# Emitting a fused sparse-attention and gated-MLP kernel in beats of one 512-wide score tile, with DMA transposes for k and x, staged q and separate PSUM banks for the MLP

## The chip, the cores and the metric

The kernel runs on one core of a Trainium2 chip. The metric is the time of one execution on the device, in microseconds (us). A core has a matrix engine (PE), a vector engine (VectorE, DVE in the profile), a scalar engine (ScalarE, ACT), a general engine (GpSimd, POOL), a queue engine (SyncE, SP) and 16 DMA engines. The order of each engine's instructions is laid out when the program is built. In the traces of this case, a wait at the head of an engine's order holds what stands behind it: VectorE, for one, stood 4.80 us before a copy whose data was late, with a ready instruction next in line (shown below).

Runs carry a state, fast or slow. A slow run is one over 1.5% above the fastest of the same kernel.

## The reference

There are 4 batches of 8 heads, 768 positions and 64 channels. Each query scores the 32-key chunks by an upper bound made from the minimum and maximum of k in the chunk, keeps the 6 best chunks, and does causal attention over them. The heads are joined to x (768 x 512 per batch), which goes through a gated MLP with a mixing step along the sequence.

```python
ub = np.sum(np.maximum(q[:, :, :, None, :] * k_min[:, :, None, :, :],
                       q[:, :, :, None, :] * k_max[:, :, None, :, :]), axis=-1)
ub = np.where(causal, ub, -1000000000.0)
top_chunks = np.argsort(ub, axis=-1)[..., -top_k:]
...
scores = np.where(mask, scale * np.matmul(q, k.transpose(0, 1, 3, 2)), -1000000000.0)
attn = softmax(scores)
x = (attn @ v), heads joined
...
h = np.maximum(x @ w_in, 0.0)                  # 512 -> 1024
u, v = h[..., :512], h[..., 512:]
v_n = (v - mean(v)) / sqrt(var(v) + 1e-06)
v_s = np.einsum('ts,bsd->btd', w_spatial, v_n) + b_spatial[None, :, None]
return (u * v_s) @ w_out
```

## The kernel before

The kernel works in 16 pairs of heads. `load` fetches the pair's k, q and v (float32 in memory, float16 in the tile) in six DMA transfers. `prep` transposes k on PE, finds chunk minima and maxima, transposes q, makes bounds, selects chunks, writes the selection into the free half of the padded q tile, and transposes both heads' query operands (`a`). `attend` makes scores in tiles of up to 1,024 columns, with the causal triangle added by a small product, takes the exp, and multiplies by the values. The MLP of batch b is cut into pieces and handed out over the pairs of batch b+1.

```python
ps_sc = ctx.enter_context(tc.psum_pool(name="ps_sc", bufs=2))    # tiles of 1024 columns: 4 banks
ps_tr = ctx.enter_context(tc.psum_pool(name="ps_tr", bufs=2))
ps_acc = ctx.enter_context(tc.psum_pool(name="ps_acc", bufs=2))  # bounds, values and the whole MLP
...
def load(i):
    for hi in range(2):
        ...
        nc.gpsimd.dma_start(out=kp[:, :, hi, :], in_=view(k))
        nc.gpsimd.dma_start(out=qs[:, :, hi, c0:c0 + D], in_=view(q))   # straight into the padded tile
        nc.gpsimd.dma_start(out=vt[:, :, hi, 0:D], in_=view(v))

def prep(i):
    tr = trans_tile()
    for t in range(NQT):
        nc.tensor.transpose(tr[:, t * P:(t + 1) * P], kp[:, t, :, :], identity)
    ... # kmm: chunk max and min of tr, on VectorE
    nc.scalar.copy(kh[0][D:2 * D, :], tr[0:D, :])
    nc.scalar.copy(kh[1][0:D, :], tr[D:2 * D, :])
    for m in range(2):
        nc.gpsimd.tensor_tensor(km[:, m], ..., op=Alu.mult)              # on POOL
    ... # q transposed, its positive and negative parts, bounds, top 8, selection
    for hi in range(2): ... # a: six transposes and a VectorE copy

def attend(i):
    for hi in range(2):
        for g, strips in enumerate(STRIPS):                              # 1024, 1024, 640 columns
            for (t, q0, n, col, dg) in strips:
                mm(sc[:, col:col + n], lhsT=kh[hi][:, t * P:(t + 1) * P], rhs=a[hi][:, q0:q0 + n], ...)
                if dg:
                    mm(sc[:, col:col + P], lhsT=identity, rhs=tri, start=False, stop=True)
            nc.scalar.activation(out=e[...], in_=sc[:, 0:WIDTHS[g]], func=Act.Exp, scale=scale)
        ... # values on PE, normalised into x16 by VectorE
    ... # six PE transposes of x16, VectorE copy into xT

load(0); load(1)
load_weights()                # w_in, w_spatial, w_out, on the POOL queue
prep(0)
for i in range(NPAIR):
    load(i + 2); prep(i + 1); attend(i)
    ... # a share of the MLP pieces of the batch before
```

The softmax here doesn't subtract the row's maximum and nothing guards it: scores larger than these inputs give would overflow.

## Time and profile before

| | before |
|---|---|
| time, median of 4 runs beside the changed kernel | 292.24 us (291.39 to 294.32) |
| span of the profiled execution | 287.5 us |
| first exp of the attention | 27.5 us |
| first exp of pair 4 (batch 1 begins) | 78.0 us |
| first MLP result (batch 0) | 86.9 us |
| first MLP result of batch 3 | 257.1 us |
| instructions on PE | 2,340 |

A result of the MLP counts from the moment when ScalarE begins to copy it out of PSUM (tile `vraw`). The time to the first MLP result of batch 0, the time from there to the first of batch 3, and the rest (the last MLP alone) divide the span into 86.9 + 170.2 + 30.4 us. The middle part is called "the twelve pairs" below, as it holds three MLPs spread over twelve pairs. It is not exactly the attention of pairs 4 to 15 (pairs are counted from 0): pair 4 has its first exp at 78.0 us, before the first MLP result.

These are lines of the page of before. The digits are the busy tenths of 40 slices of 7.2 us each. "PEclk" is the PE clock that was granted.

```profile
PE 222.4 (77%) x2340; PEld 144.9 (50%) x2340; DVE 170.7 (59%) x498; ACT 154.3 (54%) x217; POOL 98.1 (34%) x150
...
PE   0037028787879798989798989978888989799994
...
DMA  0999997879996667558984848079220000140005
...
PE 50%; ACT 23%; DMA 8%; POOL 7%; DVE 7%; issue 3%; ACTq 0%; DVEq 0%; POOLq 0%
```

No engine is full. The last line shares out the chain of waits, followed back from the end: PE and ScalarE alternate. PE's row has a zero in the fifth slice (28.8 to 36 us).

The table by stretches of the same profile gives, after each stretch's length, the busy time of each engine, then the granted PE clock, the mean busy share of the DMA engines over the stretch (as a sum of overlapping packets, so it may pass 1) and the GB/s moved.

```profile
core 0: us, PE busy (x) PEld busy (x) DVE busy (x) ACT busy (x) POOL busy (x), PEclk, DMA share, GB/s
0.00:46.00 46.00, 12.65 (x110) 9.30 (x111) 18.49 (x57) 8.23 (x9) 31.83 (x51) 0.85 1.16 112
...
207.00:257.00 50.00, 45.09 (x443) 28.19 (x440) 29.01 (x80) 29.68 (x44) 1.88 (x5) 1.00 0.10 26
257.00:287.50 30.50, 25.24 (x133) 12.67 (x130) 12.33 (x26) 10.98 (x22) 0.00 (x0) 1.00 0.18 67
```

In the stretch from 207 to 257 us, PE is busy for 45.1 of 50 us. What is missing there is waiting. From 0 to 46 us, PE does 12.7 us of work. The timeline of PE shows the hole. Each line has start, length, and in brackets how long the engine was idle before it and what released it.

```profile
28.86 0.22 PE L213 MATMUL sc<-a_213,kh_0_92 128*128 128x128 f16 x1
40.09 0.20 PE L177 MATMUL acc<-km,rq 128*128 128x48 f16 x1 [11.01 <-POOL km L161]
```

PE waits 11 us for a small product `km` on POOL, and POOL stands, in its own order, at three load issues that in the trace wait in turn for w_in, ws_raw and w_out to land (3.5, 5.4 and 1.3 us). Why loads of q, k and v have to wait for weights is not shown. The waits view adds up such waits (total, times, longest).

```profile
POOL kp L140 <- PE tr L152: 48.0, 9, 9.7
...
ACT e L217 <- PE sc L216: 42.9, 31, 12.0
```

ScalarE waits 42.9 us in all for scores (12.0 of them in the hole just shown), in a kernel where PE waits too. So for part of the time the two engines take turns rather than work side by side.

### The profile page before, as it was taken

The page shows a single profiled execution, that of the slowest core. Times are in us where ns is not written, and L with a number is a line of the kernel's source. Part 1 is how long each engine was busy: PE and PEld are TensorE (multiplying, and loading weights), DVE is VectorE, ACT ScalarE, POOL GpSimd, SP SyncE. Part 2 cuts the span into 40 slices and gives each one's busy share as a digit, 9 for nine tenths or more (in the row PEclk, how much of TensorE's full clock was granted, in tenths as well). Part 3 has the DMA queues.
Part 4 walks back from the last instruction along what each step waited for, and adds up shares of the span by engine and source line. Part 5 has one row for each costly group of instructions (what it writes and reads, how often), then busy time and mean ns, then how long its engine had stood idle before and what let it go on. Part 6 is the DMA issues. An engine that isn't in the chain of part 4 may idle for free.

```text
span 287.5 us, 5812 instructions
## 1 busy us (share of the span) xinstructions
PE 222.4 (77%) x2340; PEld 144.9 (50%) x2340; DVE 170.7 (59%) x498; ACT 154.3 (54%) x217; POOL 98.1 (34%) x150
## 2 busy tenths in 40 slices
PE   0037028787879798989798989978888989799994
PEld 0025016666655565655465656655546565544551
DVE  8337005888788875565579865474688654238330
ACT  1021405775785868146878674086878660656213
POOL 9995264546562434124243424051200000000000
PEclk9999758999999999999999999999999999999999
DMA  0999997879996667558984848079220000140005
GB/s 1 65 120 199 194 127 52 56 49 71 70 65 41 46 41 47 37 64 65 204 55 31 55 31 57 0 81 222 16 15 3 0 2 0 39 182 2 0 0 219
DMA packets 80590, 18.86 MB, mean 66 GB/s; under 512 B 75698, under 2 KB 76978, under 8 KB 80564
## 3 DMA queue, kind: packets, MB, share of 16 engines
q0 software_dynamic: 77104, 12.20, 57.3%
q1 hardware_dynamic: 3460, 6.30, 6.0%
q8 instruction: 18, 0.29, 0.4%
q14 instruction: 8, 0.07, 0.1%
HBM read 24.39 MB, written 6.29 MB: 107 GB/s over the span
## 4 chain that ended last, share of the span: by engine, by line
PE 50%; ACT 23%; DMA 8%; POOL 7%; DVE 7%; issue 3%; ACTq 0%; DVEq 0%; POOLq 0%
ACT e L217 13%; PE acc L322 11%; PE sc L213 7%; PE acc L310 7%; DMA w_out_sb<-in_moe_w_out_dram 6%; PE acc L224 5%; PE acc L333 5%; PE acc L285 5%; DVE stats L289 2%; PE tr L234 2%; POOL kp L140 2%; PE sc L216 2%; DMA out_dram<-o 2%; ACT uT L312 2%; PE acc L324 2%
## 5 line engine op out<-in xcount | busy, mean ns | idle before, releaser
L217 ACT ACTIVATE e<-sc 128x1024 f16<-128x1024 f32 (+1 forms) x96 | 84.0, 916 | 44.0 <-PE sc L216 42.9
L140 POOL DMA_DIRECT2D kp<-in_k_dram x32 | 26.7, 839 | 54.1 <-PE tr L152 48.0
L224 PEld LDWEIGHTS <-e 128*128 128x128 f16 x672 | 27.0, 98 | 31.3 <-ACT e L217 17.8
L216 PE MATMUL sc<-tri,identity 128*128 128x128 f16 x192 | 39.5, 222 | 0.0
L336 ACT COPY o<-acc 128x512 f32<-128x512 f32 x24 | 14.0, 585 | 46.9 <-PE acc L333 44.8
L322 PE MATMUL acc<-wsT,vn 128*128 128x512 f16 (+1 forms) x192 | 37.2, 325 | 0.4 <-ACT uT L312 0.2
L325 DVE TENSOR_TENSOR gT<-acc,uT 128x512 f16<-128x512 f32 (+1 forms) x32 | 17.8, 557 | 20.0 <-PE acc L324 18.8
L155 DVE TENSOR_REDUCE kmm<-tr 128x24 f16<-128x768 f16 x16 | 15.3, 953 | 20.4 <-PE tr L152 20.3
L322 PEld LDWEIGHTS <-vn 128*128 128x128 f16 x192 | 18.2, 98 | 12.2 <-issue 1.1
L310 PE MATMUL acc<-xT,w_in_sb 128*128 128x512 f16 (+1 forms) x128 | 23.4, 325 | 0.9 <-ACT uT L312 0.7
L333 PE MATMUL acc<-w_out_sb,gT 128*128 128x512 f16 x96 | 23.1, 378 | 0.4 <-ACT o L336 0.3
L216 PEld LDWEIGHTS <-identity 128*128 128x128 f16 x192 | 19.0, 99 | 7.4 <-issue 5.7
L285 PE MATMUL acc<-w_in_sb,xT 128*128 128x512 f16 x96 | 22.2, 379 | 0.0
L177 PE MATMUL acc<-km,rq 128*128 128x48 f16 x160 | 9.6, 188 | 15.9 <-POOL km L161 14.5
L152 PE MATMUL tr<-identity,kp 128*128 128x128 f16 x96 | 10.0, 229 | 14.7 <-DMA kp<-in_k_dram 14.6
L312 ACT ACTIVATE uT<-acc 128x512 f16<-128x512 f32 (+1 forms) x32 | 14.3, 488 | 12.4 <-PE acc L310 12.3
L289 DVE BATCH_NORM_STATS2 stats<-vraw 128x6 f32<-128x512 f32 x24 | 16.6, 694 | 6.1 <-ACT vraw L287 6.1
L227 DVE RECIPROCAL rec<-acc 128x6 f32<-128x6 f32 x32 | 6.1, 190 | 22.9 <-PE acc L224 22.9
L287 ACT ACTIVATE vraw<-acc 128x512 f32<-128x512 f32 x24 | 14.3, 597 | 9.6 <-PE acc L285 9.6
L180 DVE TENSOR_TENSOR acc<-acc,cmask 128x40 f32<-128x40 f32 x16 | 3.3, 208 | 25.6 <-PE acc L177 22.7
L161 POOL TENSOR_TENSOR km<-kmm,hmask 128x48 f16<-128x48 f16 x32 | 8.3, 276 | 26.3 <-DVE kmm L155 22.6
L310 PEld LDWEIGHTS <-w_in_sb 128*128 128x128 f16 x128 | 12.1, 97 | 9.7 <-issue 1.3
(236 smaller groups left out, 452.0 us busy)
## 6 DMA issues: line engine op xcount, KB each, us to landing
out_dram<-o SPq DMA_DIRECT2D x24, 256.0 KB, 2.0
kp<-in_k_dram POOLq DMA_DIRECT2D x32, 96.0 KB, 3.3
qs_90<-in_q_dram POOLq DMA_DIRECT2D x12, 96.0 KB, 3.3
vt_96<-in_v_dram POOLq DMA_DIRECT2D x12, 96.0 KB, 3.0
ws_raw<-in_moe_w_spatial_dram POOLq DMA_DIRECT2D x1, 1152.0 KB, 15.1
w_in_sb<-in_moe_w_in_dram POOLq DMA_DIRECT2D x1, 1024.0 KB, 10.3
qs_98<-in_q_dram POOLq DMA_DIRECT2D x10, 96.0 KB, 3.2
vt_104<-in_v_dram POOLq DMA_DIRECT2D x10, 96.0 KB, 3.1
```

What stands on the lines that cost most here:

```text
L140: nc.gpsimd.dma_start(out=kp[:, :, hi, :], in_=view(k))
L213: mm(sc[:, col:col + n], lhsT=kh[hi][:, t * P:(t + 1) * P], rhs=a[hi][:, q0:q0 + n], start=True, stop=not dg)
L216: mm(sc[:, col:col + P], lhsT=identity, rhs=tri, start=False, stop=True)
L217: nc.scalar.activation(out=e[:, BASES[g]:BASES[g] + WIDTHS[g]], in_=sc[:, 0:WIDTHS[g]], func=Act.Exp, scale=scale)
L224: mm(avv[:, qi, :], lhsT=e[:, c:c + P], rhs=vt[:, t, hi, 0:D + 1], start=(t == 0), stop=(t == qi))
L285: mm(hv, lhsT=x[:, ko, bi * P:(bi + 1) * P], rhs=w_in_sb[:, ko, DH:DFF], start=(ko == 0), stop=(ko == NDO - 1))
L289: nc.vector.bn_stats(stats, st["vraw"][:, bi, :])
L310: mm(hu[:, 0:t1 - t0], lhsT=w_in_sb[:, ko, db * P:(db + 1) * P], rhs=x[:, ko, t0:t1], start=(ko == 0), stop=(ko == NDO - 1))
L312: nc.scalar.activation(st["uT"][:, db, t0:t1], hu[:, 0:t1 - t0], func=Act.Relu)
L322: mm(vs[:, 0:t1 - t0], lhsT=st["vn"][:, si, db * P:(db + 1) * P], rhs=wsT[:, si, t0:t1], start=(si == 0), stop=False)
L325: nc.vector.tensor_tensor(st["gT"][:, db, t0:t1], in0=vs[:, 0:t1 - t0], in1=st["uT"][:, db, t0:t1], op=Alu.mult)
L333: mm(o_ps, lhsT=st["gT"][:, db, ti * P:(ti + 1) * P], rhs=w_out_sb[:, db, :], start=(db == 0), stop=(db == KO - 1))
```

## The change

The intent is to keep PE fed. The whole kernel is emitted in beats, one for each 512-wide score tile (12 a pair), and in each beat a small share of every other stage is placed: preparation of coming pairs up to 27 beats ahead, values, and two matmuls or so of the MLP. The parts are:

- scores in six tiles of up to 512 columns with three one-bank buffers, in place of three tiles of 1,024 with two double-bank buffers;
- k and x transposed by the DMA engines (30 of the 32 transposes), q and `a` still by PE;
- q loaded into a staging tile and placed into the padded tile by two VectorE copies, so that loads can cover four heads at once (27 transfers of q, k and v in place of 96);
- kh copies moved from ScalarE to VectorE, `a` copies from VectorE to ScalarE, `km` from POOL to VectorE;
- the causal triangle cut out of e by POOL from the second batch on, in place of products on PE;
- three PSUM banks for the MLP, one for the values, one for transposes and bounds.

```diff
-STRIPS = [
-    [(0, 0, 512, 0, True), (1, 128, 512, 512, True)],
...
+TILES = [
+    [(0, 0, 512, 0)],
+    [(1, 128, 512, 0)],
+    [(2, 256, 512, 0)],
+    [(3, 384, 384, 0), (1, 640, 128, 384)],
+    [(4, 512, 256, 0), (0, 512, 256, 256)],
+    [(5, 640, 128, 0)],
+]
...
-    ps_sc = ctx.enter_context(tc.psum_pool(name="ps_sc", bufs=2))
-    ps_tr = ctx.enter_context(tc.psum_pool(name="ps_tr", bufs=2))
-    ps_acc = ctx.enter_context(tc.psum_pool(name="ps_acc", bufs=2))
+    ps_sc = ctx.enter_context(tc.psum_pool(name="ps_sc", bufs=3))
+    ps_tr = ctx.enter_context(tc.psum_pool(name="ps_tr", bufs=1))
+    ps_acc = ctx.enter_context(tc.psum_pool(name="ps_acc", bufs=1))
+    ps_ml = ctx.enter_context(tc.psum_pool(name="ps_ml", bufs=3))
...
+        def q_place(self):
+            nc.vector.tensor_copy(self.qs[:, :, 0, D:2 * D], self.q[:, 0])
+            nc.vector.tensor_copy(self.qs[:, :, 1, 0:D], self.q[:, 1])
+
+        def k_transpose(self):
+            src = self.k.rearrange("p h t d -> p (h t d)")
+            if self.i == 0:
+                ... # on PE
+            else:
+                kT = sb.tile([P, 2, NQT // 2, P], F16, tag="kT", name="kT")
+                nc.sync.dma_start_transpose(out=kT.rearrange("d h m s -> d (h m) s"), in_=src)
...
+        def k_operand(self, hi):
+            d0, d1 = HALF[1 - hi]
+            dst = self.kh[hi][d0:d1].rearrange("d (p m s) -> d p m s", p=2, s=P)
+            for sp, (s0, s1) in enumerate(HALF):
+                nc.vector.tensor_copy(dst[:, sp], self.kT[s0:s1, hi])
...
+        def triangle(self, hi, g0):
+            if self.b == 0:
+                return                                  # batch 0: product on PE, as before
+            e = self.e[hi]
+            blk = bass.AP(e.tensor, e.offset + g0 * 512, [list(e.ap[0]), [512, 3], [1, P]])
+            nc.gpsimd.affine_select(out=blk, in_=blk, compare_op=Alu.is_ge, fill=0.0, ...)
...
+        def x_transpose(self):
+            if self.i < NPAIR - 1:
+                nc.sync.dma_start_transpose(out=dst..., in_=self.x16...)
+            else:
+                ... # on PE
...
+    for g, group in enumerate(groups):
+        if g >= 2:
+            t0 = group[0] * BEATS
+            at(t0 - 36, load, "k", g, group)
+            at(t0 - 34, load, "q", g, group)
+            at(t0 - 16, load, "v", g, group)
...
+        at(t0 - 22, p.q_place)
+        at(t0 - 27, p.k_transpose)
+        at(t0 - 22, p.k_max)
+        at(t0 - 21, p.q_transpose)
...
+        at(t0 - 12, p.select)
...
+    at(1 * BEATS, load_w_in)
+    at(2 * BEATS, load_w_spatial)
+    at(3 * BEATS, load_w_out)
...
+    for b in range(B):
+        steps = mlp(b)
+        first, count = (b + 1) * HP * BEATS + 9, HP * BEATS
+        total, done = sum(c for c, _ in steps), 0
+        for cost, fn in steps:
+            at(first + done * count // total, fn)
+            done += cost
```

## The prediction

> **What bounds it now.** No engine does. The page gives PE 77% busy, VectorE 59%, ScalarE 54% and the chain of waits alternates: PE 50%, ScalarE 23%, DMA 8%, POOL 7%. By stretches (timeline):
>
> - Start, 0 to 46 us. POOL builds masks until 8 us, then issues the first k load; PE starts at 14.6, the first exp at 27.5. PE idles from about 29 to 40: POOL, in order, holds load issues until the weight loads land (w_out takes 16.9 us), with small `km` products behind them.
> - Batch 0 attention, to 86 us: about 12 us a pair.
> - Batches 1 to 3 with the previous batch's MLP: 60, 61 and 50 us, 14.2 a pair.
> - MLP of batch 3 alone, 256 to 287.5.
>
> PE's work per pair in the third stretch, from issue intervals in the timeline (216 ns per 512 columns, 56 per transpose, 34 per 65-column product), is about 12.4 us. Nearly 2 us is waiting: bounds, values and MLP share two `acc` banks (waits view: ScalarE 42.9 us for scores).
>
> **The change, per pair with MLP (estimated).**
>
> - PE: k and x transposes leave (-0.7), triangle products become POOL selects from batch 1 (-0.64): 11.0 us.
> - ScalarE: twelve exps instead of six. 1024 columns took 1.02 us and 640 took 0.70, so 512 is 0.60 and 128 is 0.27: 6.5 us instead of 5.5. Copies of kh (2 x 0.79) leave, of a arrive. With MLP: 10.8 us.
> - VectorE: loses a copies (1.1) and x copy (0.55), gains q, kh and bounds copies (about 1.5): 10.6 us, unchanged.
> - POOL: 96 input loads become 27; four selects a pair (0.45 each), off the path unless behind an issue.
> - DMA: 30 transposes of 196 KB. None is in this trace. The Trainium skill, "VectorE: DVE Perf Modes", section "The three transpose paths", gives 1309 ns for a 128x128 block through the DMA crossbar; I estimate 3 to 5 us each. k is asked five beats before use, so hidden; x three beats before the batch's MLP, partly exposed.
>
> Three engines then sit near 11 us a pair; I expect 12.7.
>
> **Sum.** First exp at 16 us (weights later, no hole); batch 0 in 40 us (ScalarE needs 8.1 a pair plus setup); twelve pairs at 12.7, 152; drain 6; tail 28 instead of 31.5 (three MLP banks; PE needs 24.3). Span 242; the median lies some 5 us over the span: **246 us**, 8 in 10 within **228 to 266**. Faster by over 2%: 0.94; within 2%: 0.04; slower: 0.02. Two thirds of the gain comes from the start and batch 0.
>
> **What would show it.** Right: no PE hole at 29 to 40; first exp before 20 us; MLP starting before 65 us instead of 86; pair period under 13.3; PE's busy sum near 180 while ScalarE's rises to 175; transposes landing in under 6 us. Wrong: exps of 512 over 0.65 us; kT or xT leading the waits of VectorE or PE; selects behind load issues leading PE's waits before the values.
>
> **What would make it wrong.** Transposes taking 8 us or more each: 30 in one queue would set a period above 13 us, the time over 270. Four-head load issues taking four times the present 0.84 us. Fixed engine orders laid out for durations the chip doesn't have, so that three engines near 11 us wait for one another: 14 us a pair, 262. Near-perfect overlap: 230.

## The result, and the profile after

The changed kernel took 253.46 us, median of 4 runs (249.51 to 258.75; two of them slow), against 292.24 us (291.39 to 294.32) for before. The ratio of the fast runs is 0.855, with a 95% interval of 0.846 to 0.864. A ratio here is the mean time of one kernel's fast runs over the mean of the other's fast runs of the same rounds, so it is not quite the ratio of the medians quoted. The predicted 246 us is within 3% of the result, and the range of 228 to 266 holds it.

The profile first taken of the changed kernel fell in a slow run (span 257.0 us). The same kernel was therefore run again among the experiments (run a_again): 251.63 us, median of 6 (249.71 to 258.71), ratio 0.8647 [0.8586, 0.8707]. Its profile is of a fast run, and it is the profile "after" below.

| us | before | after (fast run) | predicted |
|---|---|---|---|
| first exp | 27.5 | 17.3 | 16 |
| first exp of pair 4: batch 0's attention is through | 78.0 | 65.5 | 56 |
| end of the last exp: the attention of twelve pairs is through | 251.3 | 214.0 | 208 |
| to the first MLP result of batch 0 | 86.9 | 81.4 | under 65 |
| from there to that of batch 3: "the twelve pairs" | 170.2 | 139.0 | |
| the rest | 30.4 | 27.6 | 28 |
| span | 287.5 | 248.0 | 242 |

The predicted column comes from the prediction's sum (16 + 40; twelve pairs at 12.7; a drain of 6; the tail of 28) and from its test for the MLP's start. Against its own marks, batch 0 took 48.2 us instead of 40, and the attention of the twelve pairs 148.5 us instead of 152, or 12.4 us a pair for 12.7. But that mean hides two halves: pairs 4 to 9 took 13.7 us each (65.5 to 147.8 us), and pairs 10 to 15 took 11.0 (147.8 to 214.0).

These are the lines of the page of after that answer to those of before. A slice is now 6.2 us.

```profile
PE 202.4 (82%) x2016; PEld 129.8 (52%) x2016; DVE 179.7 (72%) x608; ACT 165.6 (67%) x323; POOL 69.8 (28%) x94
...
PE   1268585449881999699987897999999999999993
...
DMA  9999999999999999799299111102421011140005
...
PE 39%; DVE 26%; DMA 24%; ACT 6%; issue 2%; POOL 1%; POOLq 0%; ACTq 0%; DVEq 0%
PE mlp L375 26%; DMA ws_raw<-in_moe_w_spatial_dram 13%; PE sc L263 6%; DMA xT<-x 5%; PE acc L285 4%; ACT e L268 3%; DVE kmm L183 3%; DVE vn L399 3%; DMA kT<-k 3%; DVE kmm L179 3%; DVE kh L197 2%; DVE km L191 2%; DVE x L293 2%; DMA k<-in_k_d
```

Two things stand out. From about 160 us on, PE's row is all nines. And DMA's share of the chain rose from 8% to 24%: the DMA engines are at nine tenths through the first 16 slices (99 us), and PE's row has holes in just that stretch. The stretches show the same:

```profile
17.00:81.00 64.00, 42.67 (x512) 31.14 (x511) 45.34 (x168) 38.24 (x76) 22.69 (x23) 0.85 2.13 143
...
181.00:220.00 39.00, 38.88 (x387) 24.61 (x386) 20.36 (x57) 31.06 (x65) 6.94 (x13) 1.00 0.16 51
220.00:248.00 28.00, 24.11 (x134) 12.85 (x132) 12.31 (x26) 11.09 (x23) 0.00 (x0) 1.00 0.20 76
```

In the stretch that answers to 207 to 257 us of before, PE now works 38.9 of 39 us, so by busy time PE is the limit there. (Busy time alone does not prove it, as the run e_lump below shows. That twelve more small products a pair cost 0.57 us a pair, in e_tri_pe, supports it.) From 17 to 81 us, no engine is over 71% busy. Three lines of PE's timeline show holes, and one of VectorE's shows what is behind the first:

```profile
46.45 0.71 PE L250 MATMUL trm<-identity,qs 128*128 128x128 f16 x5 [4.59 <-DVE qs L243]
...
52.72 1.46 PE L341 MATMUL wtr<-identity,ws_raw 128*128 128x128 f16 x12 [3.21 <-DMA ws_raw<-in_moe_w_spatial_dram]
...
80.76 4.87 PE L375 MATMUL mlp<-w_in_sb,xT 128*128 128x512 f16 x11 [3.26 <-DMA xT<-x]
```

```profile
45.81 0.26 DVE L160 COPY qs<-q 128x384 f16<-128x384 f16 x1 [4.80 <-DMA q<-in_q_dram]
45.99 0.40 DVE L243 TENSOR_TENSOR qs<-ub,max 128x240 f16<-128x240 f32 x1
46.31 0.25 DVE L161 COPY qs<-q 128x384 f16<-128x384 f16 x1
```

VectorE's next instruction was to place the q of a later pair, which had not landed. Behind it stood the selection (L243) of an earlier pair, which PE needed. (That q was issued at 18.1 us, behind k and w_in, and landed at 45.8. In the slow run the same copy waited 10.4 us.) Then PE itself had the spatial weights' transposes at the head of its order, and waited for the weights, which took 33 us from issue to landing. The third hole holds up the first MLP result: its products began at 71.5 us, but the last of them had to wait for x of pair 3, whose transpose was issued at 72.4 and landed at 80.7 us. In the listing of transfers below, the last number is the median time from issue to landing in us.

```profile
k<-in_k_dram POOLq DMA_DIRECT2D x7, 384.0 KB, 14.5
...
ws_raw<-in_moe_w_spatial_dram POOLq DMA_DIRECT2D x1, 1152.0 KB, 33.2
w_in_sb<-in_moe_w_in_dram POOLq DMA_DIRECT2D x1, 1024.0 KB, 22.3
w_out_sb<-in_moe_w_out_dram POOLq DMA_DIRECT2D x1, 512.0 KB, 36.6
...
kT<-k SPq DMA_TRANSPOSE x15, 7.0
xT<-x SPq DMA_TRANSPOSE x15, 2.5
```

The weights of before, for comparison:

```profile
ws_raw<-in_moe_w_spatial_dram POOLq DMA_DIRECT2D x1, 1152.0 KB, 15.1
w_in_sb<-in_moe_w_in_dram POOLq DMA_DIRECT2D x1, 1024.0 KB, 10.3
...
w_out_sb<-in_moe_w_out_dram POOLq DMA_DIRECT2D x1, 512.0 KB, 16.9
```

The median of 7.0 us for kT mixes two states. This is the line of the same listing for 15 to 85 us alone:

```profile
kT<-k SPq DMA_TRANSPOSE x6, 12.0
```

The idle PE costs twice. From 44.5 to 58.2 us the granted PE clock was 0.50 (0.66 on average from 40 to 60), and the 512-column score products there take 0.63 us instead of 0.38. The Trainium skill, "TensorE: Matmul & The Clock Gate", section "What's actually happening", says that after an idle window of about 3.4 us PE falls to half its clock; the hole of 4.6 us, in which the clock fell to 0.50, agrees with it.

### The profile page after: what moved, and what is told of

The parts are those of the page before. It is cut to its first block, busy times and chain, and to the rows that moved or that the text cites. A ratio compares the mean times of both kernels' runs of the same rounds, so it can differ in the third digit from the quotient of the medians.

```text
span 257.0 us, 5354 instructions
## 1 busy us (share of the span) xinstructions
PE 203.3 (79%) x2016; PEld 130.1 (51%) x2016; DVE 180.7 (70%) x608; ACT 165.8 (64%) x323; POOL 69.6 (27%) x94
## 4 chain that ended last, share of the span: by engine, by line
PE 39%; DMA 30%; DVE 20%; POOL 4%; issue 3%; ACT 3%; SPq 0%; POOLq 0%; ACTq 0%
PE mlp L375 27%; DMA q<-in_q_dram 16%; DMA kT<-k 7%; PE sc L263 5%; PE acc L285 4%; DMA k<-in_k_dram 3%; DMA xT<-x_960 3%; DVE kmm L183 2%; DVE kmm L179 2%; DVE stats L387 2%; PE tr L250 2%; ACT e L268 1%; DVE vn L399 1%; DVE rq L214 1%; DVE gT L415 1%
## 5 line engine op out<-in xcount | busy, mean ns | idle before, releaser
L268 ACT ACTIVATE e<-sc 128x512 f16<-128x512 f32 x192 | 99.4, 555 | 35.5 <-PE sc L263 28.6
L275 POOL TENSOR_SCALAR_AFFINE_SELECT e<-e 128x384 f16<-128x384 f16 x48 | 25.6, 535 | 100.5 <-ACT e L268 100.5
L375 PE MATMUL mlp<-wsT,vn 128*128 128x512 f16 (+1 forms) x192 | 42.9, 330 | 0.0
L375 PE MATMUL mlp<-w_in_sb,xT 128*128 128x512 f16 x96 | 27.3, 400 | 6.7 <-DMA xT<-x_960 3.1
L415 DVE TENSOR_TENSOR gT<-mlp,uT 128x512 f16<-128x512 f32 (+1 forms) x32 | 17.7, 555 | 12.7 <-PE mlp L375 11.9
L375 PE MATMUL mlp<-xT,w_in_sb 128*128 128x512 f16 (+1 forms) x128 | 25.8, 326 | 0.0
L375 PE MATMUL mlp<-w_out_sb,gT 128*128 128x512 f16 x96 | 25.6, 379 | 0.0
L423 ACT COPY o<-mlp 128x512 f32<-128x512 f32 x24 | 14.2, 592 | 14.7 <-PE mlp L375 13.6
L375 PEld LDWEIGHTS <-vn 128*128 128x128 f16 x192 | 18.3, 99 | 10.0 <-DVE vn L399 0.2
L385 ACT ACTIVATE vraw<-mlp 128x512 f32<-128x512 f32 x24 | 14.5, 605 | 11.4 <-PE mlp L375 11.0
L179 DVE TENSOR_REDUCE kmm<-kT 128x24 f16<-128x768 f16 x15 | 14.2, 945 | 5.0 <-DMA kT<-k 5.0
L375 PEld LDWEIGHTS <-xT 128*128 128x128 f16 x96 | 9.3, 102 | 15.9 <-DMA xT<-x_960 3.4
L315 POOL DMA_DIRECT2D k<-in_k_dram x9 | 12.1, 1348 | 17.3 <-issue 11.9
L407 ACT ACTIVATE uT<-mlp 128x512 f16<-128x512 f32 (+1 forms) x32 | 15.8, 506 | 1.4 <-PE mlp L375 1.4
L183 DVE TENSOR_REDUCE kmm<-kT 128x24 f16<-128x768 f16 x15 | 14.1, 942 | 0.0
## 6 DMA issues: line engine op xcount, KB each, us to landing
q<-in_q_dram POOLq DMA_DIRECT2D x7, 384.0 KB, 13.1
vt_82<-in_v_dram POOLq DMA_DIRECT2D x2, 384.0 KB, 14.5
vt_80<-in_v_dram POOLq DMA_DIRECT2D x2, 384.0 KB, 18.3
```

Source lines behind the costliest of these rows:

```text
L179: nc.vector.tensor_reduce(self.kmm[:, 0, :], self.kT.rearrange("d h m (c ch) -> d (h m c) ch", ch=CHUNK), axis=AX.X, op=Alu.max)
L183: nc.vector.tensor_reduce(self.kmm[:, 1, :], self.kT.rearrange("d h m (c ch) -> d (h m c) ch", ch=CHUNK), axis=AX.X, op=Alu.min, negate=True)
L268: nc.scalar.activation(out=self.e[hi][:, g * 512:g * 512 + width], in_=sc[:, 0:width], func=Act.Exp, scale=scale)
L275: nc.gpsimd.affine_select(out=blk, in_=blk, compare_op=Alu.is_ge, fill=0.0, base=0, channel_multiplier=-1, pattern=[[0, 3], [1, P]])
L315: nc.gpsimd.dma_start(out=t[:, 0:n, :, 0:D], in_=src)
L375: mm(st[group][:, 0:cols], lhsT=lhsT, rhs=rhs, start=(j == 0), stop=(j == n - 1))
```

## The experiments

Two theories of the early part (0 to 81 us):

- **T, the transposes' traffic.** The DMA transposes of k and x load the DMA engines in a stage where they have no time to spare. Everything that lands late then blocks an in-order engine. In its strong form, transposes and loads slow each other beyond the sum of their times.
- **F, the order.** The weights are asked for too early (POOL runs ahead of the beats), and the fixed orders put consumers of late data ahead of urgent work. The transposes themselves are harmless.

A third candidate stayed untested: the loads themselves were changed too, from 96 KB for one head to 384 KB for four, asked for up to 36 beats ahead (a load of k of before landed in 3.3 us at the median, one of after in 14.5). No run undid that alone.

The further experiments ask which parts made the twelve pairs short, and what limits the best version. One caution holds for all of them: each engine's order is laid out anew when the program is built, from the builder's own estimate of durations. A small edit can therefore move other instructions too. With the MLP in lumps, for instance, a line comparison of the 2,064 products of PE in the two traces finds 1,070 lines that differ from its parent's (a moved product counts twice), most of them by intent; in the last experiment, 124 differ.

### probe: the DMA stages alone (wrong result on purpose)

```diff
+    phase(0, 2, 0, 0)    # (number, w_in loads, q loads, transposes), each waits for the one before
+    phase(1, 0, 4, 0)
+    phase(2, 0, 0, 6)
+    phase(3, 2, 0, 6)
+    phase(4, 0, 4, 6)
+    phase(5, 1, 2, 0)
-    ... # the whole kernel; the output is zeros
```

> A kernel that only moves data, in six stages one after the other: 2 loads of w_in alone; 4 loads of four heads of q alone; 6 transposes of 128x768 alone; 2 loads of w_in with 6 transposes; 4 loads of q with 6 transposes; 1 load of w_in with 2 of q. The output is zeros on purpose. Theory T (transposes and cast loads slow each other down on the same 16 DMA engines): the mixed stages take clearly longer than the sum of their parts alone, by a factor of 1.5 or more, and packets of the loads that take 32 ns alone take 100 ns or more. Theory F (the transposes are cheap and only the order in the load queue matters): a mixed stage takes about as long as the sum of its parts or less.

Measured (one run, 119.04 us, state unknown): two w_in loads alone 14.1 us; four q loads alone 13.6 us; six transposes alone 9.35 us, or 1.56 us each. Two w_in loads with six transposes took 18.45 us (sum of the parts 23.4), and four q loads with six transposes 21.0 us (sum 22.9). These are the listings for the three stages that have transposes, in that order: alone, with w_in, with q.

```profile
t<-s SPq DMA_TRANSPOSE x6, 2.6
```

```profile
w<-in_moe_w_in_dram POOLq DMA_DIRECT2D x2, 1024.0 KB, 12.1
t<-s SPq DMA_TRANSPOSE x6, 9.4
```

```profile
q<-in_q_dram POOLq DMA_DIRECT2D x4, 384.0 KB, 14.3
t<-s SPq DMA_TRANSPOSE x6, 8.4
```

The strong form of T falls for the probe: a mixed stage takes no longer than its parts one after the other, and the 128-byte packets of the q loads take 32 ns on average alone and beside the transposes, where T asked for 100 or more. But a transpose that lands in 2.6 us alone takes 8.4 to 9.4 us at the median beside loads, and one took 14.5. So the traffic adds up, and each transfer's latency grows with what is in flight. How much a transpose adds is better read from the mixed stages than from the 1.56 us, because alone the six were issued only every 1.3 us: six of them added 4.4 us to the w_in loads and 7.4 us to the q loads, or 0.7 to 1.2 us each. This agrees with the Trainium skill, "DMA: Bandwidth & Descriptors": section "Issuing engines are not separate DMA queues" says that all DMAs run on the same 16 engines and interleave, and section "Queues, rings and completion order" says that each engine goes round its queues packet by packet. The longer landings fit both; the turn from packet to packet itself is not shown by a run here.

### a_pe_early: the early transposes back on PE

```diff
+K_DMA_FROM = 5
+X_DMA_FROM = 4
...
+            elif self.i < K_DMA_FROM:
+                tr = ps_ml.tile([P, S], F16, tag="mlp", name="ktm")
+                for t in range(NQT):
+                    nc.tensor.transpose(tr[:, t * P:(t + 1) * P], src[:, t * P:(t + 1) * P], identity)
+                kT = sb.tile([P, 2, NQT // 2, P], F16, tag="kT", name="kT")
+                nc.scalar.copy(kT.rearrange("d h m s -> d (h m s)"), tr)
...
-            if self.i < NPAIR - 1:
+            if X_DMA_FROM <= self.i < NPAIR - 1:
```

> The changed kernel, but k of the first five pairs and x of the first four are transposed on TensorE (k copied out by ScalarE, x by VectorE), so that no DMA transpose runs while the weights load. Theory T: the weight loads land by about 45 us instead of 74, the load of q for pairs 2 and 3, which ended at 77 us, lands before 45, the 25 us between the first exps of pairs 2 and 3 of batch 0 shrinks to about 10, and the time falls by 12 to 20 us, to about 235. Theory F (the weights stand in the queue ahead of q whatever runs beside them): the hole stays over 15 us and the time changes by less than 5 us.

Measured: 236.74 us (236.21 to 239.34), ratio 0.817 [0.8111, 0.8228]. This was the fastest version with an interval. The first MLP result comes at 68.3 us instead of 81.4, and all the rest is as in after: 138.7 us for the twelve pairs and 27.5 us for the tail. Between the first exps of pairs 2 and 3, 8.0 us passed instead of 19.0 in after, as T expected.

```profile
DVE 47%; PE 37%; ACT 7%; DMA 5%; issue 2%; POOL 0%; ACTq 0%; DVEq 0%; POOLq 0%
...
ws_raw<-in_moe_w_spatial_dram POOLq DMA_DIRECT2D x1, 1152.0 KB, 20.0
w_in_sb<-in_moe_w_in_dram POOLq DMA_DIRECT2D x1, 1024.0 KB, 14.2
w_out_sb<-in_moe_w_out_dram POOLq DMA_DIRECT2D x1, 512.0 KB, 21.1
```

DMA's share of the chain fell from 24% to 5%. The weights, issued within 2.4 us of the same moments, landed in 14, 20 and 21 us instead of 22, 33 and 37. Eight transposes left the early part (k of pairs 1 to 4, x of pairs 0 to 3). At the 0.7 to 1.2 us each that they added in the probe, that is an estimated 6 to 10 us of DMA time; the first MLP result came 13.1 us earlier. So T is right that these transposes cost time, but the probe's sum does not give all of it. The rest can be late data at the head of an order, or a slowdown in the kernel that the probe did not have: from 15 to 85 us the 128-byte load packets of after took 42.8 ns on average, against 31.9 in before and 36.5 here (the median was 32 in all three). No run separates the two.

### a_k_early: only k back on PE

```diff
 K_DMA_FROM = 5
-X_DMA_FROM = 4
+X_DMA_FROM = 0
```

> The changed kernel with only k of the first five pairs on TensorE; all x stay DMA transposes. If the latency of kT under the weight loads is what holds the first pairs, nearly all of the 14 us that both together gave comes back: about 238. If it is the amount of DMA work (30 transposes sharing the engines with loads) each transpose counts alike and about half comes back: 243 to 245.

Measured: 240.82 us (237.77 to 243.67; two of the four runs slow), ratio 0.8225 [0.8158, 0.8292]; first MLP result at 71.9 us. Four of the eight transposes brought 9.5 us of the 13.1. So k may count for more than its number: its consumers stand further ahead in VectorE's order. But the intervals of the two runs overlap, and the share of x is not settled.

### a_w_late: the DMA transposes kept, the weights later

```diff
+    def gate(tile_ap, i):                       # the load then has to follow an exp of pair i
+        nc.scalar.copy(tile_ap, pairs[i].e[0][0:1, 0:1])
     def load_w_in():
+        gate(w_in_sb[0:1, 0, 0:1], 2)           # w_spatial: pair 3, w_out: pair 4
...
-    at(1 * BEATS, load_w_in)
-    at(2 * BEATS, load_w_spatial)
-    at(3 * BEATS, load_w_out)
+    at(2 * BEATS + 1, load_w_in)
+    at(3 * BEATS + 1, load_w_spatial)
+    at(4 * BEATS + 1, load_w_out)
...
-        at(4 * BEATS + 2 * so, prep_w_spatial, so)
+        at(5 * BEATS + 2 * so, prep_w_spatial, so)
```

> The changed kernel with the three weight loads held back until pairs 2, 3 and 4 have begun (a one-element write by ScalarE that each load must follow), all DMA transposes kept. Theory F: q and k of pairs 2 to 5 are no longer behind the weights, the hole between pairs 2 and 3 closes and the time falls by 10 us or more. Theory T: the transposes slow the weights just the same when they come later, so the hole moves to pairs 4 to 6 (the MLP of batch 0 begins later than at 90 us) and the time changes by less than 6 us.

Measured: 243.16 us (242.33 to 243.52), ratio 0.8369 [0.832, 0.8419]; first MLP result at 74.9 us. All transposes stay on the DMA engines, and still about 8 us are gained (ratio 0.837 against 0.865), between what F and T expected. So F holds too, in part: the early weights were in the way of the loads. The edit also moves PE's own transposes of w_spatial twelve beats later, so the place of that consumer and the traffic are not separated. The k loads of the stretch from 15 to 85 us landed in 13.4 us at the median instead of 18.9, and the q loads in 16.1 instead of 24.5. The transposes gained less (kT 8.3 us instead of 12.0, xT 9.6 instead of 8.3 in that stretch), and 6.4 us to a_pe_early remain. Both results fit one shortage: too many bytes asked of the DMA engines before 80 us. Whichever of them is put elsewhere, the wait shrinks. Weights later and transposes on PE together were not run.

A count supports that. From 15 to 85 us, before moved 7.06 MB at 101 GB/s on average, and after 10.06 MB at 144 GB/s. Of the 3 MB more, 1.97 MB are transposes, and the rest are loads asked for further ahead. The count alone does not decide: in the same stretch a_pe_early moved 10.58 MB and a_w_late 10.75 MB, and both were faster. What is asked for first counts too.

### a_again: the changed kernel once more

No edit.

> The changed kernel unchanged, for a profile of a fast run and a closer time. The first profile fell in a slow run. Expected: 249 to 252 us in fast runs; the hole between the first exps of pairs 2 and 3 is there in the fast run too, at 12 us or more (if it is under 10, it belonged to the slow run alone and the early transposes are not what the fast runs lose).

Measured: 251.63 us, as given above; the four fast runs lie between 249.71 and 252.9. The hole between the first exps of pairs 2 and 3 is 19.0 us. The parts of its span are the "after" of this document.

### a_pe_all: no DMA transposes at all

```diff
-K_DMA_FROM = 5
-X_DMA_FROM = 4
+K_DMA_FROM = 16
+X_DMA_FROM = 16
```

> The changed kernel without any DMA transpose: k (copied out by ScalarE) and x (by VectorE) on TensorE for all pairs. Theory T: the same gain at the start as with the first pairs alone; later, where loads are few, the added 0.7 us of TensorE and 0.8 us of ScalarE a pair cost at most 0.7 us a pair, 8 us in all: about 235 to 243, still below the changed kernel's 250. Theory F: no gain at the start and 8 us lost later: 255 to 262.

Measured: 241.09 us (239.97 to 241.62), ratio 0.8297 [0.8252, 0.8341]. The first MLP result comes at 67.5 us, as in a_pe_early (68.3), but the twelve pairs take 143.7 us instead of 138.7; a late pair takes about 12.4 us instead of 11.3. So the later DMA transposes are worth some 4.4 us. The early ones had cost some 13 us, and as emitted all of them together were a net loss of about 10 us (ratio 0.865 against 0.830).

### e_tri_pe: triangles on PE in all batches

This and the following runs start from a_pe_early.

```diff
-                diag = self.b == 0 and si == 0
+                diag = si == 0
...
-            if self.b == 0:
+            if True:
                 return                          # no selection on POOL
```

> The version with early transposes on TensorE, with the triangle products on TensorE in all batches as in batch 0, no selects on POOL. Twelve products of 54 ns a pair: if TensorE bounds the last pairs (11.3 us a pair), these go to 11.9 and the time rises by about 4 us, to 241, less where VectorE bounds. If the selects' latency costs more than the products, the time falls.

Measured: 243.09 us (242.15 to 243.18), ratio 0.8362 [0.832, 0.8404]. That is 6.4 us more, and the twelve pairs take 145.6 us instead of 138.7: 0.57 us a pair for 12 small products each. The time rose, so the selections on POOL, at 0.54 us each, are the cheaper way here.

### e_lump: the MLP in one lump a pair

```diff
-            at(first + done * count // total, fn)
+            at(first + BEATS * (done * count // total // BEATS), fn)
```

> The version with early transposes on TensorE (236.7 us), with the MLP's steps emitted in lumps of a quarter of a batch at the start of each pair instead of spread over its twelve beats. If the even spread is what brought the pairs with MLP from 14.2 us (before) towards TensorE's 11, the last pairs lengthen from 11.3 to 13 us or more and the time rises by over 10 us. If the order inside a pair matters little (the pairs are bound by the engines' sums), the time stays within 4 us.

Measured: 248.56 us (245.7 to 251.94), ratio 0.8562 [0.8473, 0.8651]. This is the largest effect in the steady part: the twelve pairs take 153.4 us instead of 138.7. Pairs 10 to 14 take 11.2 to 13.4 us instead of 10.2 to 11.5, and not all of them the 13 or more that were expected. The work is the same. Here is the stretch of the third MLP in a_pe_early, and then in e_lump:

```profile
168.00:207.00 39.00, 38.88 (x381) 24.41 (x379) 20.34 (x57) 30.94 (x65) 6.97 (x13) 1.00 0.20 53
...
176.00:220.00 44.00, 42.80 (x402) 25.62 (x401) 21.43 (x69) 30.13 (x65) 6.77 (x13) 1.00 0.22 51
```

Over the three stretches from MLP to MLP, PE is idle 14.4 us instead of 8.4 in a_pe_early, and busy 139.6 us for 1,361 products instead of 130.6 for 1,356. So some 6 us are added waiting, and some 9 us are products that count as busy for longer. PE's busy time runs from issue to a modelled end, so products that don't follow each other closely count for more; that reading of the 9 us was not tested.

### e_shared: values and MLP in one ring of four banks

```diff
-    ps_acc = ctx.enter_context(tc.psum_pool(name="ps_acc", bufs=1))
-    ps_ml = ctx.enter_context(tc.psum_pool(name="ps_ml", bufs=3))
+    ps_ml = ctx.enter_context(tc.psum_pool(name="ps_ml", bufs=4))
...
-                av = ps_acc.tile([P, 512], F32, tag="acc", name="acc")
+                av = ps_ml.tile([P, 512], F32, tag="mlp", name="acc")
```

> The version with early transposes on TensorE, with the attention values in the same ring of four PSUM banks as the MLP, instead of one bank for values and three for the MLP. If banks of its own matter to the MLP, groups of values, which stay in their bank for about four beats, hold MLP groups up in order and the pairs with MLP lengthen by 0.5 us or more: over 6 us in all. If not, the time stays within 3 us.

Measured: 237.21 us, median of 4 (234.24 to 239.47), of which two were slow. No interval was given. The two fast runs, 234.24 and 234.99, over the mean 289.12 of the six fast runs of before in the same rounds, make 0.811, against 0.817 for a_pe_early. Banks of its own for the MLP show no gain, with this order of emission.

### e_q_direct: q straight into the padded tiles

```diff
         def q_place(self):
-            nc.vector.tensor_copy(self.qs[:, :, 0, D:2 * D], self.q[:, 0])
-            nc.vector.tensor_copy(self.qs[:, :, 1, 0:D], self.q[:, 1])
+            src = q[self.b, 2 * self.hp:2 * self.hp + 2].rearrange("h (so si) d -> si h so d", si=P)
+            nc.gpsimd.dma_start(out=self.qs[:, :, 0, D:2 * D], in_=src[:, 0])
+            nc.gpsimd.dma_start(out=self.qs[:, :, 1, 0:D], in_=src[:, 1])
...
-            at(t0 - 34, load, "q", g, group)
+            at(t0 - 34, pairs[group[0]].q_place)
+            at(t0 - 34, pairs[group[1]].q_place)
...
-        at(t0 - 22, p.q_place)
```

> The version with early transposes on TensorE, with q loaded straight into its zero-padded tiles as in the kernel before (two loads a pair), so VectorE's two placing copies (0.3 to 0.48 us each) go. If VectorE's sum, 99% busy from 10 to 120 us, sets the pace there, ten pairs gain up to 0.8 us each: 229 to 233. If the direct loads wait for their tiles on POOL and hold selects and other loads up, the gain is lost: 236 or more.

Measured: 237.91 us (237.04 to 240.19), ratio 0.8239 [0.8167, 0.831]. No difference is shown. The first MLP result came earlier (65.1 us against 68.3), and the twelve pairs took 143.6 us instead of 138.7: POOL, which issues these loads, then waited 22 us in all for PE to have read the old q (13.2, 4.5 and 4.3 us). The staging copies buy freedom from that wait, and pay for it in VectorE time. From the first exp of pair 5 to that of pair 6 only 12.0 us passed here, against 19.0 in a_pe_early, and pair 6 began at 79.5 us instead of 81.9; pairs 7 and 9 then took longer.

### e_pool_kh: the kh copies on POOL

In a_pe_early VectorE is 98% busy from 40 to 115 us and leads the chain with 47%. The next two runs take work off it, to see whether it is the limit of pairs 5 to 9, which still take 12 to 19 us.

```diff
-                nc.vector.tensor_copy(dst[:, sp], self.kT[s0:s1, hi])
+                (nc.gpsimd if self.i else nc.vector).tensor_copy(dst[:, sp], self.kT[s0:s1, hi])
```

> The version with early transposes on TensorE (236.7 us), and the four half copies of k into its score operands moved from VectorE to POOL, except in pair 0. If VectorE (99% busy from 60 to 115 us there) sets the 13 us a pair of the first MLP stage, the periods of pairs 6 to 9 fall by about 1.3 us each and the time falls by 3 to 6 us. If not (POOL blocked behind load issues[...]), the time stays within 1.5 us or rises.

Measured: 241.86 us (240.45 to 245.48), ratio 0.8311 [0.8255, 0.8367], about 5 us slower. A copy took 503 ns on POOL, against 342 on average on VectorE in a_pe_early. POOL had to wait 11.3 us in all for score products before it could overwrite the operands, and behind those waits stood loads and triangle selections. From the first exp of pair 6 to that of pair 9, 46.1 us passed (15.9 + 14.0 + 16.2), against 41.8 (13.1 + 13.3 + 15.4).

### e_kh_act: the kh copies of pairs 6 to 10 on ScalarE

```diff
-                nc.vector.tensor_copy(dst[:, sp], self.kT[s0:s1, hi])
+                (nc.scalar.copy if 6 <= self.i <= 10 else nc.vector.tensor_copy)(dst[:, sp], self.kT[s0:s1, hi])
```

> The kernel with the early transposes on PE (236.74 us, ratio 0.817), with one further change: for pairs 6 to 10 the four operand copies of kh (64x384, 270 ns each on VectorE) are made by ScalarE. VectorE theory: after the early transposes are gone, VectorE, 98% busy from 40 to 115 us, sets the pace of pairs 5 to 9; taking 5 x 4 x 0.27 = 5.4 us off it brings 3 to 5 us, so about 233 us and a ratio near 0.805, with the periods of pairs 5 to 9 adding up to 3 to 5 us less than the 72.8 us of that kernel. Rival: PE's and ScalarE's fixed orders set the pace there and VectorE is only busy early with work that could wait; then the time stays within 1.5 us of 236.7, or rises, as ScalarE gets some 1.8 us more in each of those pairs. VectorE's busy share from 85 to 115 us should drop below 95% under the first theory only if PE then becomes the limit.

Measured: 245.49 us (244.14 to 247.11, 6 runs), ratio 0.8416 [0.8372, 0.8459], nearly 9 us slower. This is a clear miss for what was expected of it. Pair 6 began at 89.9 us instead of 81.9, and from there to pair 10 both kernels take 53.7 us. The copies are made well ahead of their pairs, so 14 of the 20 fell before 89.9 us, in the very stretch that became longer. The waits of 60 to 130 us tell why:

```profile
PE mlp L383 <- ACT vraw L393: 3.6, 1, 3.6
ACT kh L205 <- DMA kT<-k: 3.5, 1, 3.5
```

ScalarE now had the copies of a late kT at the head of its order. The MLP results behind them were not cleared from PSUM, and PE waited 3.6 us for that. An earlier wait of ScalarE, of 2.35 us up to 57.7 us, has the same releaser. A copy also took 510 ns on ScalarE, against 342 on average on VectorE in a_pe_early (the 270 of the expectation is from after). So in these runs the consumers of a DMA transpose held up whichever engine had them, and the kernel was fastest with them on VectorE. Since PE's order also changed in places, not all of the 9 us is proved to be this. And since the new waits are larger than the relief of VectorE, neither run settles whether VectorE's load limits pairs 5 to 9; that stays open.

## Why the prediction was right or wrong

**Right: the direction, and nearly the total.** 246 us were predicted, and about 252 measured. By the prediction's own marks, batch 0 came out 8 us too long and the twelve pairs 3.5 us too short. The second number is itself the mean of six pairs that took 1.0 us more than predicted and six that took 1.7 us less, so the hit on the total owes something to luck.

**Right: the start.** First exp at 17.3 us for 16 predicted, and the DMA engines are at nine tenths from the first slice on, where before they stood at zero. The hole from 29 to 40 us is gone. Others took its place, at 42 to 46 and 49 to 53 us.

**Wrong: "weights later, no hole", "batch 0 in 40 us", and "Two thirds of the gain comes from the start and batch 0".** This is the step that failed. Batch 0 took 48.2 us from its first exp to that of pair 4, and the first MLP result came only 16 us after that, at 81.4 us, where the prediction wanted the MLP to start before 65. Of the 39.5 us of span gained, start and batch 0 gave 12.5 (78.0 to 65.5 us at pair 4), or 5.5 at the first MLP result. Two thirds (30 of 45.5 us) comes out if the 86 us of the first MLP result of before are set against the 56 us predicted for the end of batch 0's attention: those are unlike marks. The weights were not later as a whole. The prediction took their place in the beats for a time, but nothing held these three loads on POOL (it stood idle for 5.7 us in all before other loads among them), and it issued them at 15.8, 19.5 and 27.4 us, against 18.3 to 19.9 us before; only w_out came later. On top of them came loads asked for further ahead and the transposes. The DMA engines were then at nine tenths or more to 99 us, the weights took twice as long to land, and VectorE and PE stood behind late data. a_pe_early takes eight transposes out of that stage and gets 13.1 us back; a_w_late moves the weights and gets 6.5 (81.4 to 74.9 us).

**Wrong: "I estimate 3 to 5 us each ... k is asked five beats before use, so hidden".** Alone a transpose lands in 2.6 us, so the estimate was even high; in the busy stage the median of kT was 12.0 us. Five beats, less than half a pair's period, don't hide that. The figure that the prediction took from the Trainium skill ("VectorE: DVE Perf Modes", "The three transpose paths", 1309 ns for 128x128) comes with nothing on other traffic, and the runs show that the traffic beside it decides. For x the prediction had "partly exposed", and it was: in after the first MLP result waited for the transpose of pair 3's x. The prediction's own warning, "Transposes taking 8 us or more each", came true for the early part only, and so did not set every period.

**Right as a mean only: twelve pairs at 12.7 us.** They took 12.4 us on average by their exps, 13.7 in the first half and 11.0 in the second. The prediction allowed 1.7 us a pair of mutual waiting over PE's estimated 11.0. There was next to none of it in the end: from 181 to 220 us PE worked 38.9 of 39 us. The experiments name what the parts are worth: the even spread of the MLP (14.7 us of the twelve pairs), the triangles on POOL (6.9) and the late transposes by DMA (5.0), each undone alone. These were measured on a_pe_early and need not add up, and the effects of the 512-wide tiles with three banks and of the larger loads were not isolated. Separate banks and staged q, two parts named in the change, showed no gain.

**Wrong in arithmetic: PE's busy sum of 180 us.** It was 202.4. The prediction's own savings, 1.34 us a pair over 16 pairs, take 21 from 222.4 and give 201. ScalarE came to 165.6 for 175.

**Right in the pieces:** exps of 512 columns 0.61 us (0.60), of 128 columns 0.29 (0.27); POOL selections 0.54 (0.45) and off the path; four-head load issues 1.4 us, and not four times 0.84; the tail 27.6 us (28).

**Open.** What sets the 19 us from pair 5 to pair 6, and the 13 to 15 us of pairs 6 to 8, of a_pe_early: VectorE leads the chain there, but moving the kh copies off it in two ways made things slower, and loading q directly, which also takes work off it, shortened the first and not the whole. And of the 13.1 us that the early transposes cost, 3 to 7 us are more than the probe's sum explains.

## What to carry to other kernels

Before moving work to the DMA engines, look at how busy they are in the stage where it will run, and not over the whole kernel: here the later transposes were worth some 4 us, and the early ones cost 13 us while weights and first inputs came in. A place in the order of emission is not a time; an engine with nothing to wait for issues its loads at once, so a load that should come later needs something that it has to wait for. A consumer of prefetched data placed far ahead in an engine's order turned a late transfer into a stall of what stood behind it. And spreading work evenly in small pieces was worth 14.7 us here against the same work in one lump a pair. Last, compare like marks: a prediction that sets the first MLP result of one kernel against the end of the attention in the other finds a gain that is not there.

## What the Trainium skill lacked or had wrong

- "VectorE: DVE Perf Modes", "The three transpose paths", gives one figure for the DMA transpose (1309 ns for 128x128) and none for its latency beside other traffic. Here a transpose of 128x768 landed in 2.6 us alone, at a median of 8.4 to 9.4 us beside loads in the probe, and 12.0 us in the kernel's busy stage. Six blocks in 2.6 us also show that the 1309 ns are not a cost per block.
- "Advanced Engine Details and Errata", "X-Bar Transpose (TRN2)", says that transpose DMAs are as fast as regular ones and expects 350 to 400 GB/s. Six of 196,608 bytes from one queue took 9.35 us, 126 GB/s on average (peaks of 292 in 0.24 us slices). They were issued only about every 1.3 us, so this is the pace of the issues: the run neither reaches the figure nor refutes it. The loads that turn float32 into float16 were no faster in the probe (1.57 MB written in 13.6 us, 116 GB/s), which agrees with the comparison.
- "DMA: Bandwidth & Descriptors", "Issuing engines are not separate DMA queues", agrees with the runs but gives no size. Mixed stages took 18.45 us for parts of 23.4, and 21.0 for parts of 22.9, so a sum of the parts was an upper bound here.
- No page that I read gives durations for these: a VectorE copy of 64x24 float16 elements, 272 ns on average over the run of after, no less than one of 64x384 (266 ns; in a_pe_early the two averaged 237 and 342 ns, so the size does not fix them); that second copy on ScalarE, 510 ns (e_kh_act), and on POOL, 503 ns (e_pool_kh); a triangular selection of 128x384 on POOL, 0.54 us; the issue of a load on POOL, 0.84 us for 768 rows and 1.4 us for 3,072; the issue of a 128x768 transpose on the SyncE queue, 1.2 to 1.3 us.
